# Float64 weights of a three-stage chain turned into float32 ahead of their pass and kept in main memory

## The chip, the cores and the metric

One core of one Trainium2 chip runs the whole program. The metric is the device time of one execution in microseconds (us). The time of the kernel before is the median of its runs shown below.

## What is computed

Three layers in a row. A retention layer comes first: for 4 batches and 8 heads, `scores = q k^T / 8`, times a decay matrix `gamma^(i-j)` on and below the diagonal, times `v`. Its output, reshaped to 2304 tokens by 512 columns, goes through two feed-forward layers:

```python
def _moe_ref(x, w_in, w_out):
    h = x @ w_in                    # 2304x512 @ 512x2048
    g = h * np.cos(h)
    return (g @ w_out).astype(np.float32)

def _moe2_ref(x, w_in, w_out):
    h = x @ w_in
    g = np.maximum(h, 0.0) + np.log1p(np.exp(-np.abs(h)))
    return (g @ w_out).astype(np.float32)
```

q, k and v are float32. The four weight matrices are float64. The engines have no float64 arithmetic, so the kernel has to turn every weight into float32 from its bits. Each float32 factor is then split into a high and a low part in TensorE's reduced float32 format, and a product is three matmuls: high by high, high by low, low by high.

## The kernel before, in words

**Weights.** A layer's 2048 hidden columns are 16 blocks of 128 (index `f`). A block has two tiles, `z = 0` (its columns of `w_in`) and `z = 1` (its rows of `w_out`), each 128 x 512 values, 512 KB in float64. `convert` (L327) makes one tile float32. A DMA (L339) brings the 512 KB into a buffer `wr`, of which there are three. ScalarE scales the high words into `wy` (L344). For layer 2 and for blocks 0 to 7 of layer 1, ScalarE also extracts the top bits of the low words (L350), and VectorE assembles the result in `wk` with two operations (L356, L363). For blocks 8 to 15 of layer 1, VectorE does it with three (L359, L363, L367). There are two buffers `wk` and one `wy`. Then ScalarE writes the high part, and VectorE or GpSimd subtracts to get the low part.

**First part (`moe_a`).** The attention is cut into 64 pieces. 16 of them run alone at the start; the others lie between the matmuls of the first feed-forward layer's blocks 0 to 7, which go over five groups of tokens (512, 512, 384, 384, 512). The weights of these blocks are converted one block at a time (`weight`, L380). Their partial sums go to main memory (`pd`).

**Second part (`moe_c`), three passes.** Pass 0 takes blocks 8 to 15 of layer 1, pass 1 blocks 0 to 7 of layer 2, pass 2 blocks 8 to 15 of layer 2. Each pass goes over the tokens in five pieces of 512, 512, 512, 512 and 256 (in an order of its own), and over its eight blocks as four pairs. `quad` (L832) computes two blocks at once by Strassen's scheme in Winograd's form: seven products of half size with sums and differences in PSUM (L890 to L898). `weight_pair` (L404) prepares a pair: four converted tiles (L428, L452), four combinations (L445), six splits into high and low (L424, L425, L453, L455). A pass's pair occupies the same SBUF slot as the pair of the same number in the pass before, so it can only be written once that pair has been used for the last time, and must be written before the new pass reaches it, four pairs later. The input `x` of a piece is loaded, combined and split by `x_load_c` (L1018), and in pass 1 its parts are stored for pass 2.

**Order.** Every operation is registered with a duration and a due time (`key`). `Plan.order` (L141) simulates the engines and takes, again and again, the operation that can start first; among those that can start at the same moment the smaller key goes first. That fixes each engine's program order. An operation marked "pool or dve" or "act or dve" goes to whichever engine gives the smaller start plus `FLEX` (or `FLEX_AD`) times duration (L178 to L186). A DMA is issued by SyncE (SP), in order, not before its key minus `LEAD` in the plan. Buffers of a ring (`wr`, `wk`, `tt`, and so on) are handed out in the order in which the operations were registered. The constants at the top (L68 to L108) set the keys: `W0` and `M0` for the start of the first part, `W2` and `W3` for pairs, `XC` for loads of `x`.

Of the kernel before, what the change touches and what calls it, by code (L numbers as in the profile page):

```python
# [7 lines left out]
F32 = mybir.dt.float32  # L8
F32R = mybir.dt.float32r
I32 = mybir.dt.int32  # L10
# [6 lines left out]
NF = DFF // 128  # L17
# [6 lines left out]
NM = len(GROUPS)  # L24
# [40 lines left out]
    return layer == 2 or f < FA  # L65


FLEX = 0.27  # L68
FLEX_AD = 0.824
NP = 3  # L70
RS = 5
WR = 3
# [1 line left out]
PT = 3  # L74
R0 = 22.0
WB = (21.627, 3.294)
W2 = (18.111, 6.589, 14.31, 1.214)
W3 = (16.671, 1.958)
XC = 3.809
LAG_C = 1.049  # L80
TT = 3
TURN = 0.6
XS = 60.0
FILL = (2, 5)
EARLY = 12.734
EARLY_2 = 8.236
AHEAD = {}
GAP = 2.0
LO_A = "pool or dve"
# [4 lines left out]
WARM = 350  # L94
DX = 20.621
LEAD = 7.381
W0 = (39.65, 2.003, 3.451)
M0 = 28.787
AK = (1.0, 2.2)
PAIR_A = 0.959  # L100
ALONE = 4
LENT = (0, 2)
SPREAD = (4, 6, 6)
# [141 lines left out]
def retention_moe_moe(ctx, tc, qkv, w1, w2, mask, mtail, dq, dk, out):  # L245
    nc = tc.nc
    pool = lambda name, bufs=1, **kw: ctx.enter_context(tc.tile_pool(name=name, bufs=bufs, **kw))
    dram = pool("dram", space=bass.MemoryType.DRAM)
    psum = pool("psum", 1, space=bass.MemoryType.PSUM)
    stage = pool("stage", 1)  # L250
# [18 lines left out]
    yd = dram.tile([128, NC, NT], F32, name="yd")  # L269
    sd = [dram.tile([128, len(CB), 7, 512], F32, name=f"sd{g}") for g in "hl"]  # L270
    od = dram.tile([NT, DM], F32, name="od")
    m_t = cst.tile([128, 4, 2, 128], F32, name="m_t")
    mt_t = cst.tile([128, 4, 64], F32, name="mt_t")
    dq_t = cst.tile([128, 4, 320], F32, name="dq_t")
# [2 lines left out]
    T = {}  # L277

    def dma(dst, src, nbytes, key, r=(), w=(), new=(), pre=None):
        def go():  # L280
            if pre:
                pre()
            nc.sync.dma_start(dst(), src())

        op("sp", 0.45, key, go, r, w, new, nbytes=nbytes)
# [41 lines left out]
    def convert(layer, f, z, k):  # L327
# [49 lines left out]
            op("dve", t_dve(512), k + 0.8, bits3, r=[rk, ak], w=[ak], port=True)  # L377
        return ak, lambda: T["wk", u].bitcast(F32)

    def weight(layer, f, key, step):  # L380
        wk = ("w", layer, f)
        for z in range(2):
            k = key + z * step
            ak, val = convert(layer, f, z, k)

            def hi(z=z, val=val):
                if z == 0:
                    T[wk] = tuple(wa_of(f).tile([128, 1024], F32R, tag=f"{g}{f}", name=g) for g in ("wh", "wl"))
                s = slice(z * 512, z * 512 + 512)
                nc.scalar.activation(T[wk][0][:, s], val(), AF.Copy)  # L390

            def lo(e, z=z, val=val):
                s = slice(z * 512, z * 512 + 512)
                sub(e, T[wk][1][:, s], val(), T[wk][0][:, s])

            th, tl = (wk, "h", z), (wk, "l", z)
            op("act", t_act(512), k + 2.2, hi, r=[ak], w=[th],
               new=[(f"w{f}", 1, wk)] if z == 0 else [])
            if LO_A == POOL_DVE:
                op(POOL_DVE, 512, k + 2.8, lo, r=[ak, th], w=[tl])  # L400
            else:
                op("pool", t_pool(512), k + 2.8, lambda lo=lo: lo(nc.gpsimd), r=[ak, th], w=[tl], port=True)

    def weight_pair(layer, q, key, step):  # L404

        slot_ = q % (NP2 // 2)
        wk = ("wp", layer, q)  # L410
        made = (wk, "made")

        def make():
            p = wp["qqrp"[slot_]].tile([128, 5632], F32R, tag=f"pair{slot_}", name="pair")
            T[wk] = p[:, 0:1792], p[:, 1792:3584]
            T[wk, "o"] = p[:, 3584:5632].rearrange("p (j g d) -> p j g d", j=2, g=2)

        op("host", 0.0, key, make, r=[("qqrp"[slot_] + "open",)], w=[made], new=[(f"wp{slot_}", 1, wk)])
        val, ak = [None, None], [None, None]
        part = lambda g, a, b: T[wk][g][:, a * 256:b * 256]  # L420

        def split(name, a, b, k, src, r):
            n = (b - a) * 256
            op("act", t_act(n), k, lambda: nc.scalar.activation(part(0, a, b), src(), AF.Copy), r=r + [made], w=[(wk, "h", name)])  # L424
            op(POOL_DVE, n, k + 0.6, lambda e: sub(e, part(1, a, b), src(), part(0, a, b)), r=r + [(wk, "h", name)], w=[(wk, "l", name)])  # L425

        for j in range(2):
            ak[j], val[j] = convert(layer, 2 * q + j, 0, key + j * step)  # L428
        k = key + step + 2.2
        split("a", 0, 2, key + 2.2, val[0], [ak[0]])  # L430
        split("b", 2, 3, k, lambda: val[1]()[:, 256:512], [ak[1]])
        tt = [("tt", wk, z) for z in range(2)]
        at = lambda i: T[tt[i // 2]][:, i % 2 * 256:i % 2 * 256 + 256]
        A = lambda: val[0]()
        Bv = lambda: val[1]()
        t_ = lambda i: (tt[i // 2], i % 2)
        for i, (x, y, o_, r) in enumerate((
                (lambda: Bv()[:, 0:256], lambda: Bv()[:, 256:512], ALU.add, [ak[1]]),
                (lambda: at(0), lambda: A()[:, 0:256], ALU.subtract, [ak[0], t_(0)]),
                (lambda: A()[:, 0:256], lambda: Bv()[:, 0:256], ALU.subtract, [*ak]),  # L440
                (lambda: A()[:, 256:512], lambda: at(1), ALU.subtract, [ak[0], t_(1)]))):
            def combine(e, x=x, y=y, o_=o_, i=i):
                if i % 2 == 0:
                    T[tt[i // 2]] = wp["q"].tile([128, 512], F32, tag="tt", name="tt", bufs=TT)
                e.tensor_tensor(at(i), x(), y(), o_)  # L445

            op(POOL_DVE, 256, k + 0.1 * i, combine, r=r + [("qopen",)], w=[t_(i)], new=[] if i % 2 else [("tt", TT, tt[i // 2])])
        for name, a in (("c", 3), ("d", 5)):
            split(name, a, a + 2, k + 0.6, lambda a=a: T[tt[a // 2 - 1]], [t_(a - 3), t_(a - 2)])
        for j in range(2):  # L450
            k = key + (2 + j) * step
            ok, ov = convert(layer, 2 * q + j, 1, k)  # L452
            op("act", t_act(512), k + 2.2, lambda j=j, ov=ov: nc.scalar.activation(T[wk, "o"][:, j, 0], ov(), AF.Copy),  # L453
               r=[ok, made], w=[(wk, "oh", j)])
            op(POOL_DVE, 512, k + 2.8, lambda e, j=j, ov=ov: sub(e, T[wk, "o"][:, j, 1], ov(), T[wk, "o"][:, j, 0]),  # L455
               r=[ok, (wk, "oh", j)], w=[(wk, "ol", j)])
# [657 lines left out]
    def moe_c(ph, y):  # L1114
# [9 lines left out]
        for m in range(n // 128 if ph else NC):  # L1124
# [20 lines left out]
            for i, (p, q) in enumerate(cuts):  # L1145
# [2 lines left out]
            dma(lambda r0=r0, m=m: out[r0:r0 + 128] if ph else yd[:, m, a:a + n], lambda pk=pk: T[pk], 512 * w, K + 1,  # L1148
                r=[(pk, i) for i in range(len(cuts))], w=[("out", r0) if ph else ("yd", m, b)])

    x_of[0, 0] = x_load_c(0, 0, CO[0][0], MB - XC)
    for q in range(half_p):
        weight_pair(1, half_p + q, M[NM - 2] + W2[0] + W2[1] * q if q < 2 else MB + q * UC(512) - W2[2], W2[3])
    for ph in range(3):
        if ph == 1:
            op("act", 1.3, CM[1][0], lambda: nc.scalar.preload_act_table_set("softplus"), r=[("sin",)], w=[("ln",)])
        if ph:
            x_of[ph, 0] = x_load_c(ph, 0, CO[ph][0], CM[ph][0] - XC)
            for q in range(half_p):
                weight_pair(2, q + (ph - 1) * half_p, CM[ph][0] + q * UC(512) - W3[0], W3[1])  # L1160
        for y in range(len(CB)):
            moe_c(ph, y)
    plan.emit(nc)
# [66 lines left out]
```

## Time and profile before

| | us |
|---|---|
| runs of the kernel before | 892.19, 896.02, 897.17 |
| median | 896.02 |
| the profiled execution, its own time | 892.48 |
| its span, first to last instruction | 890.7 |
| outside the span | 1.8 |

The profiled execution is one more execution than the three runs. Its span is cut into its parts by rows of the trace further down. In the profile, PE is TensorE's matmuls, PEld its weight loads, DVE VectorE, ACT ScalarE, POOL GpSimd, SP the queue that issues the DMAs. A granted clock of 1.00 is TensorE's full 2.4 GHz. In a row of matmuls, times in square brackets are the idle time of the engine before that row and what ended it.

### The profile page before, as it was taken

Reading aid. Unit: us, or ns where it says so; the run is one execution under the profiler, and the core shown is the slowest. Engines: PE = TensorE matmul, PEld = TensorE weight load, DVE = VectorE, ACT = ScalarE, POOL = GpSimd, SP = SyncE. Lnnn points to the kernel's source line nnn. Section 1 sums busy time; section 2 is a strip of 40 time slices with the busy share of each in tenths; the row PEclk is TensorE's granted clock in tenths of the full one; section 3 lists DMA queues with packets and bytes.
Section 4 is the critical chain, followed back from the end, with each engine's and each line's share of the span. In section 5 each row is a group of like instructions: output and inputs, shape, how many; then the busy total and the mean of one; then the engine's idle time right before and its main releaser. Section 6 shows DMA issues by size and latency. Waiting matters only on the chain.

```text
span 890.7 us, 15157 instructions
## 1 busy us (share of the span) xinstructions
PE 861.9 (97%) x5780; PEld 751.2 (84%) x5780; DVE 633.0 (71%) x1169; ACT 454.2 (51%) x897; POOL 170.2 (19%) x168
## 2 busy tenths in 40 slices
PE   7989999999999989999999889999999999999998
PEld 5767777899987878898888769889888888888887
DVE  3889655565499996667879996567668886565654
ACT  1469533435367865545768845335446752233322
POOL 4522000100041361113232160013003220000000
PEclk9999999999999999999999999999999999999999
DMA  9876332532256512345365607156525734421202
GB/s 321 349 243 234 108 116 98 186 111 95 89 191 198 197 48 95 95 132 176 95 249 172 194 24 309 37 226 237 220 100 214 270 126 158 164 98 71 95 29 78
DMA packets 56232, 139.13 MB, mean 156 GB/s; under 512 B 5088, under 2 KB 24672, under 8 KB 54112
## 3 DMA queue, kind: packets, MB, share of 16 engines
q1 hardware_dynamic: 56160, 138.18, 44.2%
q8 instruction: 45, 0.74, 0.3%
q14 instruction: 27, 0.22, 0.1%
HBM read 93.59 MB, written 44.56 MB: 155 GB/s over the span
## 4 chain that ended last, share of the span: by engine, by line
PE 75%; DVE 11%; DMA 5%; ACT 4%; issue 3%; SPq 1%; POOL 0%; DVEq 0%; POOLq 0%; ACTq 0%
PE acc L919 27%; PE acc L823 9%; PE o L857 8%; PE hb L857 7%; PE s L857 6%; PE ha L857 5%; PE ha L723 4%; PE hb L723 3%; PE o L636 2%; DMA wr<-in_w 2%; DVE wk L363 2%; DMA pt<-pd 1%; DVE pair L291 1%; PE s L559 1%; DVE wk L356 1%
## 5 line engine op out<-in xcount | busy, mean ns | idle before, releaser
L919 PE MATMUL acc<-pair,gh 128*128 128x512 f32 x576 | 180.8, 395 | 0.1
L919 PE MATMUL acc<-pair,gl 128*128 128x512 f32 x288 | 114.0, 396 | 2.1 <-DVE gl L291 2.1
L919 PEld LDWEIGHTS acc<-pair,gh 128*128 128x128 f32 x576 | 101.0, 189 | 16.5 <-ACT gh L802 0.6
L919 PE MATMUL acc<-gh,pair 128*128 128x512 f32 (+1 forms) x320 | 100.2, 370 | 0.3 <-ACT gh L802 0.3
L790 ACT ACTIVATE er<-er 128x512 f32<-128x512 f32 (+1 forms) x80 | 47.0, 588 | 91.0 <-DVE er L787 90.9
L857 PE MATMUL o<-xx,pair 128*128 128x256 f32 x320 | 79.4, 290 | 6.2 <-DVE o L898 3.8
L857 PE MATMUL o<-x,pair 128*128 128x256 f32 x328 | 79.8, 287 | 3.1 <-ACT cv L295 3.1
L857 PE MATMUL hb<-x,pair 128*128 128x256 f32 x328 | 78.6, 283 | 3.9 <-DVE hb L898 1.9
L857 PE MATMUL hb<-xx,pair 128*128 128x256 f32 x320 | 78.0, 286 | 0.1
L857 PEld LDWEIGHTS o<-xx,pair 128*128 128x128 f32 x320 | 57.4, 191 | 12.9 <-DVE o L898 7.1
L919 PEld LDWEIGHTS acc<-pair,gl 128*128 128x128 f32 x288 | 54.2, 188 | 16.0 <-DVE gl L291 3.4
L773 ACT ACTIVATE er<-er,hp_t 128x512 f32<-128x512 f32 (+2 forms) x80 | 54.1, 679 | 24.0 <-DVE er L770 23.1
L919 PEld LDWEIGHTS acc<-gh,pair 128*128 128x128 f32 x320 | 58.5, 188 | 9.1 <-ACT gh L802 0.5
L857 PEld LDWEIGHTS o<-x,pair 128*128 128x128 f32 x328 | 58.8, 192 | 7.8 <-ACT cv L295 4.1
L857 PEld LDWEIGHTS hb<-x,pair 128*128 128x128 f32 x328 | 57.6, 188 | 8.9 <-DVE hb L898 3.4
L823 PE MATMUL acc<-gh,wh 128*128 128x512 f32 (+1 forms) x160 | 60.4, 377 | 0.3 <-ACT gh L802 0.3
L857 PEld LDWEIGHTS hb<-xx,pair 128*128 128x128 f32 x320 | 56.4, 188 | 4.9 <-DVE hb L898 2.4
L823 PE MATMUL acc<-gl,wh 128*128 128x512 f32 (+1 forms) x160 | 59.2, 370 | 1.3 <-DVE gl L291 1.2
L919 PE MATMUL acc<-gl,pair 128*128 128x512 f32 (+1 forms) x160 | 59.3, 370 | 0.2 <-DVE gl L291 0.2
L823 PE MATMUL acc<-gh,wl 128*128 128x512 f32 (+1 forms) x160 | 58.9, 368 | 0.0
L857 PE MATMUL s<-x,pair 128*128 128x256 f32 x256 | 58.8, 282 | 0.0
L857 PE MATMUL ha<-x,pair 128*128 128x256 f32 x256 | 58.3, 280 | 0.0
(201 smaller groups left out, 2092.3 us busy)
## 6 DMA issues: line engine op xcount, KB each, us to landing
wr<-in_w SPq DMA_DIRECT2D x64, 512.0 KB, 3.6
raw<-in_qkv SPq DMA_DIRECT2D x12, 640.0 KB, 5.0
raw<-in_qkv SPq DMA_DIRECT2D x12, 512.0 KB, 6.0
od<-pt SPq DMA_DIRECT2D x18, 256.0 KB, 2.8
pt<-od SPq DMA_DIRECT2D x18, 256.0 KB, 3.4
out<-pt SPq DMA_DIRECT2D x18, 256.0 KB, 2.0
pt<-pd SPq DMA_DIRECT2D x16, 256.0 KB, 3.3
yd<-pt SPq DMA_DIRECT2D x16, 256.0 KB, 2.2
```

The source lines that it names most:

```text
L291: e.tensor_tensor(out_, a, hi.bitcast(F32), ALU.subtract)
L356: nc.vector.scalar_tensor_tensor(T["wk", u], T["wy", u], 3, T["wr", u][:, :, 0], ALU.logical_shift_left, ALU.bitwise_or)
L363: nc.vector.scalar_tensor_tensor(a, T["wy", u], -(1 << 31), a, ALU.bitwise_and, ALU.bitwise_or)
L559: nc.tensor.matmul(X()[j][:, z], k_(j, z), q_(z)[Z[j]], start=True, stop=True)
L636: nc.tensor.matmul(o_at(z)[Z[j]], lhs(j), rhs(j), start=start, stop=stop, skip_group_check=True)
L723: nc.tensor.matmul(h_[:, 0:n], lhs, rhs[:, d, 0:n], start=(k == 0), stop=(k == 3 * NC - 1))
L773: nc.scalar.activation(e["r"], e["r"], AF.Sin, bias=hp_t[:, 0:1], scale=-1.0)
L790: nc.scalar.activation(e["r"], e["r"], AF.Softplus)
L823: nc.tensor.matmul(acc[o][:, 0:n], l[:, s], e[r], start=(first and z == 0), stop=(last and z == 2))
L857: nc.tensor.matmul(out_, w_(a), x_(b), start=(start and y == 0), stop=(stop and y == 5), skip_group_check=True)
L919: nc.tensor.matmul(acc[m][:, 0:n] if layer == 1 else acc[m], l, r, start=(begin and z == 0), stop=(stop and z == 2))
```

## The change

Conversion and use of a tile come apart for ten pairs of blocks. A new helper `convert_ahead` converts a pair's four tiles with the same `convert`, and stores each as float32 in a new array `wd` in main memory (256 KB). A new helper `load_values` brings two such tiles at once (512 KB) into a `wr` buffer, and `weight_pair` takes the values from there if its new argument `ahead` is true. Done so are pairs 2 and 3 of pass 0 and all four pairs of pass 1, converted from the start of the second token group of the first part on (`M[1]`), one tile every 4.372 us by the keys, and all four pairs of pass 2, converted in pass 1, one tile every 5.526 us by the keys. Pairs 0 and 1 of pass 0 are converted at their place as before. Fourteen constants that set keys and the choice of engine get other values. The arithmetic is the same.

```diff
--- before.py
+++ after.py
@@ -65,8 +65,8 @@
     return layer == 2 or f < FA
 
 
-FLEX = 0.27
-FLEX_AD = 0.824
+FLEX = 0.317
+FLEX_AD = 1.075
 NP = 3
 RS = 5
 WR = 3
@@ -74,16 +74,17 @@
 PT = 3
 R0 = 22.0
 WB = (21.627, 3.294)
-W2 = (18.111, 6.589, 14.31, 1.214)
-W3 = (16.671, 1.958)
-XC = 3.809
-LAG_C = 1.049
+W2 = (29.96, 6.115, 14.31, 1.214)
+W3 = (16.671, 1.426)
+XC = 7.768
+LAG_C = 1.076
 TT = 3
+CA = (0.0, -5.457, 4.372, 5.526)
 TURN = 0.6
 XS = 60.0
 FILL = (2, 5)
-EARLY = 12.734
-EARLY_2 = 8.236
+EARLY = 12.574
+EARLY_2 = 6.751
 AHEAD = {}
 GAP = 2.0
 LO_A = "pool or dve"
@@ -94,10 +95,10 @@
 WARM = 350
 DX = 20.621
 LEAD = 7.381
-W0 = (39.65, 2.003, 3.451)
-M0 = 28.787
+W0 = (40.929, 2.003, 3.451)
+M0 = 28.434
 AK = (1.0, 2.2)
-PAIR_A = 0.959
+PAIR_A = 1.089
 ALONE = 4
 LENT = (0, 2)
 SPREAD = (4, 6, 6)
@@ -269,6 +270,7 @@
     yd = dram.tile([128, NC, NT], F32, name="yd")
     sd = [dram.tile([128, len(CB), 7, 512], F32, name=f"sd{g}") for g in "hl"]
     od = dram.tile([NT, DM], F32, name="od")
+    wd = dram.tile([2, NF, 2, 128, 512], F32, name="wd")
     m_t = cst.tile([128, 4, 2, 128], F32, name="m_t")
     mt_t = cst.tile([128, 4, 64], F32, name="mt_t")
     dq_t = cst.tile([128, 4, 320], F32, name="dq_t")
@@ -377,6 +379,28 @@
             op("dve", t_dve(512), k + 0.8, bits3, r=[rk, ak], w=[ak], port=True)
         return ak, lambda: T["wk", u].bitcast(F32)
 
+    def convert_ahead(layer, q, key, step):
+
+        for z in range(2):
+            for j in range(2):
+                f = 2 * q + j
+                k = key + (2 * z + j) * step
+                ak, val = convert(layer, f, z, k)
+                dma(lambda f=f, z=z: wd[layer - 1, f, z], lambda val=val: val(), 128 * 2048, k + 4, r=[ak], w=[("wd", layer, f, z)])
+
+    def load_values(layer, q, z, k):
+
+        u = (layer, q, z, "v")
+        rk = (("wr",) + u,)
+
+        def pre():
+            T["wr", u] = stage.tile([128, 512, 2], I32, tag="wr", name="wr", bufs=WR)
+
+        at = lambda: T["wr", u].rearrange("p a b -> p (a b)").bitcast(F32)
+        dma(lambda: at().rearrange("p (j d) -> p j d", j=2), lambda: wd[layer - 1, 2 * q:2 * q + 2, z].rearrange("j p d -> p j d"),
+            128 * 4096, k - 3.0, r=[("wd", layer, 2 * q + j, z) for j in range(2)], w=[rk], new=[("wr", WR, rk[0])], pre=pre)
+        return [rk] * 2, [lambda j=j: at()[:, j * 512:j * 512 + 512] for j in range(2)]
+
     def weight(layer, f, key, step):
         wk = ("w", layer, f)
         for z in range(2):
@@ -401,7 +425,7 @@
             else:
                 op("pool", t_pool(512), k + 2.8, lambda lo=lo: lo(nc.gpsimd), r=[ak, th], w=[tl], port=True)
 
-    def weight_pair(layer, q, key, step):
+    def weight_pair(layer, q, key, step, ahead):
 
 
 
@@ -424,8 +448,11 @@
             op("act", t_act(n), k, lambda: nc.scalar.activation(part(0, a, b), src(), AF.Copy), r=r + [made], w=[(wk, "h", name)])
             op(POOL_DVE, n, k + 0.6, lambda e: sub(e, part(1, a, b), src(), part(0, a, b)), r=r + [(wk, "h", name)], w=[(wk, "l", name)])
 
-        for j in range(2):
-            ak[j], val[j] = convert(layer, 2 * q + j, 0, key + j * step)
+        if ahead:
+            ak, val = load_values(layer, q, 0, key)
+        else:
+            for j in range(2):
+                ak[j], val[j] = convert(layer, 2 * q + j, 0, key + j * step)
         k = key + step + 2.2
         split("a", 0, 2, key + 2.2, val[0], [ak[0]])
         split("b", 2, 3, k, lambda: val[1]()[:, 256:512], [ak[1]])
@@ -447,9 +474,11 @@
             op(POOL_DVE, 256, k + 0.1 * i, combine, r=r + [("qopen",)], w=[t_(i)], new=[] if i % 2 else [("tt", TT, tt[i // 2])])
         for name, a in (("c", 3), ("d", 5)):
             split(name, a, a + 2, k + 0.6, lambda a=a: T[tt[a // 2 - 1]], [t_(a - 3), t_(a - 2)])
+        if ahead:
+            oks, ovs = load_values(layer, q, 1, key + 2 * step)
         for j in range(2):
             k = key + (2 + j) * step
-            ok, ov = convert(layer, 2 * q + j, 1, k)
+            ok, ov = (oks[j], ovs[j]) if ahead else convert(layer, 2 * q + j, 1, k)
             op("act", t_act(512), k + 2.2, lambda j=j, ov=ov: nc.scalar.activation(T[wk, "o"][:, j, 0], ov(), AF.Copy),
                r=[ok, made], w=[(wk, "oh", j)])
             op(POOL_DVE, 512, k + 2.8, lambda e, j=j, ov=ov: sub(e, T[wk, "o"][:, j, 1], ov(), T[wk, "o"][:, j, 0]),
@@ -1148,16 +1177,21 @@
             dma(lambda r0=r0, m=m: out[r0:r0 + 128] if ph else yd[:, m, a:a + n], lambda pk=pk: T[pk], 512 * w, K + 1,
                 r=[(pk, i) for i in range(len(cuts))], w=[("out", r0) if ph else ("yd", m, b)])
 
+    for i, (layer, q) in enumerate([(1, half_p + 2), (1, half_p + 3)] + [(2, q) for q in range(half_p)]):
+        convert_ahead(layer, q, M[1] + CA[0] + 4 * i * CA[2], CA[2])
     x_of[0, 0] = x_load_c(0, 0, CO[0][0], MB - XC)
     for q in range(half_p):
-        weight_pair(1, half_p + q, M[NM - 2] + W2[0] + W2[1] * q if q < 2 else MB + q * UC(512) - W2[2], W2[3])
+        weight_pair(1, half_p + q, M[NM - 2] + W2[0] + W2[1] * q if q < 2 else MB + q * UC(512) - W2[2], W2[3], q >= 2)
     for ph in range(3):
         if ph == 1:
             op("act", 1.3, CM[1][0], lambda: nc.scalar.preload_act_table_set("softplus"), r=[("sin",)], w=[("ln",)])
         if ph:
             x_of[ph, 0] = x_load_c(ph, 0, CO[ph][0], CM[ph][0] - XC)
             for q in range(half_p):
-                weight_pair(2, q + (ph - 1) * half_p, CM[ph][0] + q * UC(512) - W3[0], W3[1])
+                weight_pair(2, q + (ph - 1) * half_p, CM[ph][0] + q * UC(512) - W3[0], W3[1], True)
+            if ph == 1:
+                for q in range(half_p):
+                    convert_ahead(2, half_p + q, CM[1][0] + CA[1] + 4 * q * CA[3], CA[3])
         for y in range(len(CB)):
             moe_c(ph, y)
     plan.emit(nc)
```

## Rows read from the trace of the kernel before

**Rows 1.** the page, section 1: span, and each engine's busy time
```profile
span 890.7 us, 15157 instructions
PE 861.9 (97%) x5780; PEld 751.2 (84%) x5780; DVE 633.0 (71%) x1169; ACT 454.2 (51%) x897; POOL 170.2 (19%) x168
```

**Rows 2.** busy by stage: length; PE, PEld, DVE, ACT, POOL (xcount); clock; DMA share; GB/s
```profile
60.00:100.00 40.00, 39.25 (x213) 31.26 (x213) 36.51 (x67) 32.38 (x61) 7.63 (x7) 1.00 0.57 191
100.00:240.00 140.00, 140.00 (x1026) 122.90 (x1026) 75.45 (x177) 56.65 (x121) 7.41 (x11) 1.00 0.33 109
...
260.00:340.00 80.00, 75.84 (x427) 66.21 (x426) 75.99 (x129) 57.76 (x105) 28.38 (x24) 0.98 0.41 138
...
440.00:460.00 20.00, 18.12 (x114) 15.92 (x114) 16.83 (x24) 11.94 (x23) 10.81 (x9) 1.00 0.45 169
...
480.00:540.00 60.00, 53.50 (x308) 46.08 (x307) 57.57 (x90) 43.08 (x81) 21.61 (x21) 0.97 0.41 133
540.00:660.00 120.00, 120.00 (x766) 107.88 (x765) 78.52 (x134) 52.72 (x106) 14.68 (x10) 1.00 0.52 199
660.00:740.00 80.00, 77.44 (x471) 67.30 (x470) 67.46 (x112) 49.61 (x96) 20.11 (x18) 1.00 0.52 188
```

**Rows 3.** the same view, L363 alone (its time and count of VectorE), by stage
```profile
60.00:100.00 40.00, 7.52 (x11) 1.00 0.57 191
...
480.00:540.00 60.00, 8.55 (x11) 0.97 0.41 133
540.00:660.00 120.00, 1.36 (x2) 1.00 0.52 199
```

**Rows 4.** timeline of TensorE at stalls: start, duration, instruction, idle before
```profile
318.68 0.58 PE L857 MATMUL o<-x,pair 128*128 128x256 f32 x1 [2.74 <-ACT cv L295]
...
504.63 0.50 PE L919 MATMUL acc<-pair,gl 128*128 128x512 f32 x1 [1.57 <-DVE gl L291]
...
530.89 0.58 PE L857 MATMUL o<-xx,pair 128*128 128x256 f32 x1 [3.16 <-DVE o L898]
...
710.80 0.39 PE L857 MATMUL hb<-x,pair 128*128 128x256 f32 x1 [1.19 <-ACT cv L295]
```

**Rows 5.** timeline of VectorE ahead of two of these stalls
```profile
503.29 0.68 DVE L363 SCALAR_TENSOR_TENSOR wk<-wy,wk 128x512 int32<-128x512 int32 x1
...
525.69 1.78 DVE L363 SCALAR_TENSOR_TENSOR wk<-wy,wk 128x512 int32<-128x512 int32 x1
...
528.72 1.77 DVE L291 TENSOR_TENSOR pair<-wk,pair 128x512 fp32r<-128x512 f32 x1
530.41 0.42 DVE L898 TENSOR_TENSOR o<-o,c 128x256 f32<-128x256 f32 x1
```

**Rows 6.** timeline of GpSimd beside them
```profile
525.18 1.74 POOL L291 TENSOR_TENSOR xx<-tt,x 128x512 fp32r<-128x512 f32 x1
```

**Rows 7.** granted clock (after the engines' busy time) in 4 us stretches behind stalls
```profile
320.00:324.00 4.00, 4.00 (x22) 3.74 (x22) 3.12 (x7) 2.12 (x5) 2.90 (x3) 0.73 0.00 0
...
532.00:536.00 4.00, 4.00 (x17) 3.28 (x17) 3.14 (x7) 1.41 (x4) 0.00 (x0) 0.78 0.44 131
```

**Rows 8.** operations of a conversion: count, shortest/median/longest in ns, first and last start
```profile
L344 ACT ACTIVATE wy<-wr x64: 644/668/692, 36.2 to 722.6; 128x512 f32<-128x512 f32 x64
L350 ACT ACTIVATE wr<-wr x48: 650/673/720, 36.8 to 717.8; 128x512 int32<-128x512 uint8 x48
L356 DVE SCALAR_TENSOR_TENSOR wk<-wy,wr x48: 670/684/1680, 38.7 to 723.4; 128x512 int32<-128x512 int32 x48
...
L363 DVE SCALAR_TENSOR_TENSOR wk<-wy,wk x64: 672/683/1776, 39.4 to 724.3; 128x512 int32<-128x512 int32 x64
```

**Rows 9.** timeline of ScalarE and SP at two places
```profile
709.33 0.66 ACT L350 ACTIVATE wr<-wr 128x512 int32<-128x512 uint8 x1 [1.32 <-DMA wr<-in_w]
...
29.65 10.08 SPq L283 DMA_DIRECT2D wr<-in_w  x5
```

**Rows 10.** issues of DMAs: KB each, median us from issue to landing
```profile
wr<-in_w SPq DMA_DIRECT2D x64, 512.0 KB, 3.6
```

## The prediction

> **What bounds the kernel now.** I read the page first: TensorE is busy in 861.9 of a span of 890.7 us, so nothing can win more than what TensorE loses [rows 1]. Then I read busy time by stage, to see where it loses [rows 2]. From 100 to 240 us (the first part) and from 540 to 660 us (inside pass 1) it is busy for the whole stretch. It is idle at the changes of pass: 80 - 75.84 = 4.2 us from 260 to 340 (into pass 0), 60 - 53.50 = 6.5 us from 480 to 540 (into pass 1), 80 - 77.44 = 2.6 us from 660 to 740 (into pass 2), and 1.9 us from 440 to 460. VectorE is at 95%, 96% and 84% in the first three (75.99 of 80, 57.57 of 60, 67.46 of 80), against 54% and 65% in the two quiet stretches. So the kernel is bound by TensorE, and by VectorE where a pass begins. The start, up to 60 us, where attention runs alone, is hardly touched by the change.
>
> What stands in VectorE's queue at those places comes from the timelines. TensorE waits 1.57 us for `gl`, and a conversion (L363) is the operation just ahead of it; it waits 3.16 us for the addition L898, and ahead of that stands another L363 that took 1.78 us [rows 4, 5]. Into pass 0 it waits 2.74 us, into pass 2 1.19 us for a copy on ScalarE; ahead of the latter a conversion (L350) had itself waited for its weights to land [rows 4, 9]. After the two longest waits the granted clock is 0.73 and 0.78 over 4 us: TensorE, idle just before, runs part of the stretch at 1.2 instead of 2.4 GHz [rows 7]. That costs another 4 x 0.27 = 1.1 and 4 x 0.22 = 0.9 us.
>
> **The change, part by part.**
>
> *Removed at the changes of pass.* A tile of layer 2 costs ScalarE 0.67 + 0.67 and VectorE 0.68 + 0.68 us [rows 8]. From 480 to 540 there are 11 conversions, 11 x 1.37 = 15 us of VectorE's 57.6 [rows 3]; without them it stands near 42 of 60, 71%. Into pass 0 only pairs 2 and 3 (8 tiles) leave; pairs 0 and 1 stay and bunch as before.
> - Into pass 0 I take the 2.74 us wait and its clock loss, 2.74 + 1.1 = 3.8. The other 1.4 us of idle time stays.
> - Into pass 1 I take the two waits that have a conversion ahead of them and the clock loss, 1.57 + 3.16 + 0.9 = 5.6. The rest, 1.8 us, stays.
> - Into pass 2 I take all, 2.6 us, since nothing but weights is prepared there (pass 2 loads finished parts of x).
> - From 440 to 460 I take nothing: there the input of pass 1 is loaded.
>
> Together 12.0 us. The bounds are 0 (another operation takes each place) and all idle time of these stages with the clock losses, 4.2 + 1.9 + 6.5 + 2.6 + 2.0 = 17.2.
>
> *Added in the first part: 24 conversions.* 8 tiles of layer 1 (three VectorE operations; I use 0.68 for each, which is high for one of them) and 16 of layer 2 make 8 x 2.0 + 16 x 1.37 = 38 us on VectorE within 24 x 4.372 = 105 us, 36% on top of 54%: 90%. ScalarE gets 8 x 0.67 + 16 x 1.34 = 27 us, 26% on top of 40%. The cover is the slack between a block's activations and its output matmuls. The nearest row is the stretch from 60 to 100 us, where the same code converts 11 tiles beside the same matmuls, with VectorE at 36.51 of 40, 91% [rows 2, 3]. TensorE is idle there 0.75 us, so at most 0.75/11 = 0.07 us per tile; the lower bound is 0. I take the upper, 24 x 0.07 = 1.6 us, as the load is as high.
>
> *Added in pass 1: 16 conversions.* 16 x 1.37 = 22 us on VectorE over 16 x 5.526 = 88 us, 25% on top of 65%, again 90%. Two conversions already lie in that stretch at no idle time [rows 2, 3]. I take 0.07 again: 1.1 us. Without cover each operation would cost TensorE its 0.68 us; that is a rival below.
>
> *Added DMAs: 40 stores of 256 KB and 20 loads of 512 KB, 21 MB in all.* The 64 loads from the inputs stay, but 40 of them move. In the first part the conversions bring 24 x 0.75 MB in 105 us, 180 GB/s on top of 109, where the queue is busy at 0.33; the stretch from 60 to 100 carries 191 at 0.57 [rows 2]. At the changes of pass a pair now needs two loads instead of four, each 3.6 us by the row of the old ones [rows 10]: a gain, in the sum above. SP issues in order, so behind a store that waits for its conversion stand attention's inputs (issued 22 us early), the partial sums `pd` and the `xd` stores, for which three buffers `pt` wait. I cost that at 0: an input has 22 us, and SP has gaps. If the cover is gone, an accumulator is emptied late, which is in the slower rival.
>
> *Keys.* `W0` delays the first weight loads by 1.28 us. The first is issued at 29.65 us [rows 9], and its key minus 3 minus `LEAD` is 39.65 - 3 - 7.38 = 29.27, so this delay will show; but a block's matmuls come only behind the attention that runs alone. I take 0, with 1.3 either way. `FLEX` shifts flexible subtractions from GpSimd to VectorE, `XC` brings x 4 us earlier, pairs 0 and 1 of pass 0 come 12 us later but wait for x's buffers anyway. The trace of before cannot price these; 2 us either way, and 0 taken.
>
> **Sum.** -12.0 + 1.6 + 1.1 = -9.3 us. The profiled execution took 892.48 us, 1.8 more than its span. The runs took 892.19, 896.02 and 897.17. The four fall in two pairs, so I put the sum on the middle of the four, (892.48 + 896.02)/2 = 894.25, which is 1.8 below the median: 894.3 - 9.3 = 885.0 us.
>
> **A rule against part of it.** While GpSimd runs an x subtraction of 1.74 us, VectorE's operations take 1.78 instead of 0.68 us: L363, but also the pair's subtraction (L291, 1.77), which the change does not remove [rows 5, 6]. The Trainium skill, page "SBUF — State Buffer", section "Who interferes with whom", says that a VectorE instruction with two SBUF inputs contends with a GpSimd instruction that reads SBUF, and that the one who comes second is blocked fully. The trace agrees: 1.1 us lost each time. By that rule taking out conversions leaves the other collisions, which is the first rival.
>
> **Rivals.**
> - *The collisions stay.* Splits and x loads still meet GpSimd's work. Then each of the two long waits shrinks only by one collision, 1.1 us, the 1.57 us wait by two conversions of 0.68 (1.4), the clock losses stay, and pass 2 gains its 2.6: 6.2 - 2.7 = 3.5 us, 890.8. For it: two of the four long operations around the 3.16 us wait are not conversions. Against it: with VectorE at 71% the queue has gaps that absorb 1.1 us. Chance 0.20.
> - *The conversions don't get away from the change of pass.* Tiles of pass 2 follow pass 1's pairs in the `wr` ring. Pair 3's last load is due at 2 x 1.426 + 3 x 10.47 - 16.67 = 17.6 us after the pass begins (10.47 is the plan's time for a pair, L309), the first conversion at -5.5. So four tiles are late by then, and with older keys than the pass's own work they go first, in a burst where VectorE was full. Then the 5.6 us are not won: 3.7 us, 890.6. Against it: a burst of 4 is less than the 11 there now. Chance 0.10.
> - *Slower: conversions break the chain of the first part.* Until the third group ends only two PSUM banks hold the hidden values (L962), and matmul, activation, split and output matmul follow each other closely. If every one of the 40 tiles puts one operation of 0.68 us in front of that chain, or a late store holds `pd`, the cost is 40 x 0.68 = 27 us, less 12.0: 894.3 + 15.2 = 909.5. It turns slower by over 0.5% when a tile costs TensorE more than (12.0 + 900.5 - 894.3)/40 = 0.46 us. Against it: 0.07 in the row. For it: in that row the converted tiles were needed at once; here 24 extra ones come on top of pieces of attention with their own deadlines. Chance 0.13.
>
> **How the numbers follow.** The forecast has 0.57. 0.5% is 4.5 us, about what a measurement of this kernel can tell from no change: faster is below 891.5, slower above 900.5. The two rivals near 890.7 hold 0.30; with the spread of the runs 0.18 of it counts as faster and 0.12 as within 0.5%. Of the slower rival 0.11 ends above 900.5 and 0.02 within. So faster 0.75, same 0.14, slower 0.11. The range reaches down to the bound of all idle time won, 894.3 - 17.2 - 1 (part of the keys' 2) = 876, and up past the small-gain rivals by the spread of the runs, to 895; the slower rival is left out.
>
> **What would show it.** Right: by stage, L363's time disappears from 480 to 540 and 660 to 740 and appears between 90 and 210; TensorE's idle time there falls from 6.5 to about 2 and from 2.6 to about 0; the clock stays at 1.00 behind the change of pass; the first part, 100 to 240, stays within 2 us of full. Wrong: a stall at L898 or `cv` with VectorE operations of 1.7 us beside GpSimd (first rival); L363 bunched in the first 40 us of pass 1 (second); matmuls L723 or L823 waiting for VectorE, or evictions waiting for `pt`, in the first part (third).

## The result, and the profile after

The changed kernel takes 883.9 us (median of 7 runs, 882.68 to 889.66) against 894.56 (7 runs, 892.19 to 897.17): a ratio of 0.9889, 95% interval 0.986 to 0.9918. The forecast was 885.0 us, faster, in a range from 876 to 895.

The traced execution of the changed kernel is the slowest of its seven (889.66 us), while that of the kernel before (892.48) lies below its median. So the two traces differ by 2.8 us where the medians differ by 10.7: what the traces show place by place is real, but they cannot be added up to the whole gain.

The page, section 1, of the changed kernel (answers to [rows 1]):

```profile
span 887.9 us, 15301 instructions
PE 865.3 (97%) x5780; PEld 751.1 (85%) x5780; DVE 630.7 (71%) x1179; ACT 454.4 (51%) x892; POOL 171.1 (19%) x163
```

Busy time by stage, columns as in [rows 2]:

```profile
100.00:240.00 140.00, 137.71 (x989) 118.80 (x988) 102.47 (x224) 80.30 (x161) 6.76 (x9) 0.98 0.68 232
260.00:340.00 80.00, 78.71 (x442) 67.81 (x441) 66.60 (x115) 53.94 (x101) 29.65 (x25) 1.00 0.36 122
...
480.00:540.00 60.00, 57.34 (x346) 50.04 (x345) 50.67 (x78) 37.60 (x69) 28.13 (x22) 0.97 0.68 236
540.00:660.00 120.00, 119.01 (x743) 105.82 (x743) 84.90 (x148) 59.06 (x115) 17.92 (x13) 1.00 0.60 219
660.00:740.00 80.00, 79.50 (x491) 70.22 (x490) 58.17 (x92) 36.79 (x72) 15.47 (x14) 1.00 0.42 154
```

At the changes of pass TensorE's idle time falls from 4.16 to 1.29, from 6.50 to 2.66 and from 2.56 to 0.50 us. In the first part it rises from 0 to 2.29, with VectorE at 102 instead of 75 us and the DMA share at 0.68 instead of 0.33.

The last operation of a conversion (L363 before, L365 now) alone, its VectorE time and count by stage (answers to [rows 3]):

```profile
100.00:240.00 140.00, 17.98 (x26) 0.98 0.68 232
480.00:540.00 60.00, 6.17 (x7) 0.97 0.68 236
540.00:660.00 120.00, 7.31 (x10) 1.00 0.60 219
660.00:740.00 80.00, 0.00 (x0) 1.00 0.42 154
```

**What was lost in the first part.** The chain of waits, 128 to 153 us (start, duration, what):

```profile
128.66 4.91 DMA wr<-in_w
...
136.43 6.03 DMA wd<-wk
...
142.72 9.69 DMA wd<-wk
...
152.51 0.70 DVE wk L358
...
153.24 0.69 DVE wk L365
153.93 0.61 DVE er L792
```

The timelines of SP, ScalarE and TensorE at that place, in this order:

```profile
141.56 0.33 SPq L285 DMA_DIRECT2D wr<-in_w  x1
...
151.78 0.67 ACT L352 ACTIVATE wr<-wr 128x512 int32<-128x512 uint8 x1 [3.67 <-DMA wr<-in_w]
152.35 0.58 ACT L788 ACTIVATE ek<-ha 128x512 int32<-128x512 f32 x1
...
157.16 0.50 PE L852 MATMUL acc<-gh,wh 128*128 128x512 f32 x1 [1.90 <-ACT gh L831]
158.06 0.50 PE L852 MATMUL acc<-gl,wh 128*128 128x512 f32 x1 [0.40 <-DVE gl L293]
```

And what the stretches around it carry (columns as in [rows 2]):

```profile
145.00:150.00 5.00, 5.00 (x24) 4.13 (x23) 3.32 (x8) 2.22 (x5) 0.25 (x1) 1.00 1.03 404
...
155.00:160.00 5.00, 2.71 (x11) 1.53 (x10) 3.98 (x8) 3.35 (x6) 0.00 (x0) 0.92 0.82 283
160.00:165.00 5.00, 5.00 (x33) 3.73 (x33) 3.96 (x10) 3.09 (x7) 0.87 (x1) 0.50 0.79 231
165.00:170.00 5.00, 5.00 (x44) 4.09 (x42) 3.42 (x7) 2.38 (x5) 0.00 (x0) 0.89 0.88 300
```

Stores of finished tokens `x`, attention's inputs and conversions fall together; the queue is full (share 1.03, 404 GB/s). The load of weights issued at 141.56 us lands 10.2 us later, and the 256 KB store issued at 142.72 takes 9.69 us. Two engines stop for them, each in its own program order. ScalarE stands 3.67 us before a conversion's L352, until the weights have landed, with the `ek` of a block (L788) queued behind it. VectorE cannot run a conversion's L358 before the store has freed a buffer `wk`, and the same block's `er` (L792) is queued behind that conversion. VectorE's is the later of the two, and the chain of waits goes through it. TensorE waits 1.90 and 0.40 us for that block's `gh` and `gl`, which is all its idle time from 155 to 160 us and in the whole first part (2.29). Then it runs from 160 to 165 us at 0.50, that is 1.2 GHz: 5 x 0.50 = 2.5 us more.

**What stayed at the change of pass.** The timelines of VectorE, GpSimd and TensorE there (answer to [rows 4 to 6]):

```profile
513.36 1.78 DVE L293 TENSOR_TENSOR xx<-tt,x 128x512 fp32r<-128x512 f32 x1
515.06 1.74 DVE L365 SCALAR_TENSOR_TENSOR wk<-wy,wk 128x512 int32<-128x512 int32 x1
516.72 0.42 DVE L927 TENSOR_TENSOR hb<-hb,c 128x256 f32<-128x256 f32 x1
...
514.55 1.71 POOL L293 TENSOR_TENSOR xx<-tt,x 128x512 fp32r<-128x512 f32 x1
...
517.20 0.39 PE L886 MATMUL hb<-xx,pair 128*128 128x256 f32 x1 [2.02 <-DVE hb L927]
```

One stall of 2.02 us is left. Its conversion is one of the tiles of pass 2. Its two slow VectorE operations, 1.78 and 1.74 instead of 0.68 us, lie beside GpSimd operations (one of 1.62 us, then the one shown, 1.71). The Trainium skill, page "SBUF — State Buffer", section "Who interferes with whom", has a VectorE instruction with two SBUF inputs contend with a GpSimd instruction that reads SBUF; the trace agrees again.

DMA issues (KB each, median us from issue to landing; answers to [rows 10]):

```profile
wr<-in_w SPq DMA_DIRECT2D x64, 512.0 KB, 4.9
wd<-wk SPq DMA_DIRECT2D x40, 256.0 KB, 4.4
wr<-wd SPq DMA_DIRECT2D x20, 512.0 KB, 3.7
```

### The profile page after: what moved, and what is told of

It is laid out like the page before. It is cut to its first block, busy times and chain, and to the rows that moved or that the text cites. A ratio compares the mean times of both kernels' runs of the same rounds, so it can differ in the third digit from the quotient of the medians.

```text
span 887.9 us, 15301 instructions
## 1 busy us (share of the span) xinstructions
PE 865.3 (97%) x5780; PEld 751.1 (85%) x5780; DVE 630.7 (71%) x1179; ACT 454.4 (51%) x892; POOL 171.1 (19%) x163
## 4 chain that ended last, share of the span: by engine, by line
PE 70%; DVE 13%; DMA 7%; ACT 5%; issue 3%; SPq 1%; POOL 1%; DVEq 0%; POOLq 0%; ACTq 0%
PE acc L948 28%; PE o L886 8%; PE hb L886 7%; PE acc L852 6%; PE s L886 6%; PE ha L886 5%; PE ha L752 2%; DMA wd<-wk 2%; PE hb L752 2%; DVE wk L365 2%; DMA wr<-in_w 2%; DVE wk L358 1%; DVE pair L293 1%; DVE gl L293 1%; DVE er L792 1%
## 5 line engine op out<-in xcount | busy, mean ns | idle before, releaser
L346 ACT ACTIVATE wy<-wr 128x512 f32<-128x512 f32 x64 | 42.8, 669 | 31.2 <-DVE wk L365 26.2
```

Source lines behind the costliest of these rows:

```text
L346: nc.scalar.activation(y, T["wr", u][:, :, 1].bitcast(F32), AF.Copy, scale=2.0 ** -112)
```

## The experiments

Short diffs go from the changed kernel. Since one execution is traced and executions differ by some us, each run has two readings: the median, and the length of each stage of its trace. The stage lengths below (us) run from start to start of the first matmul of a kind, so they are worked out from rows of TensorE's timeline: A from the first block matmul of the first layer to the fifth token group, B from there to the first `quad`, then pass 0 up to the first output matmul of layer 2, pass 1 to the middle of layer 2's output matmuls, and pass 2 to the last of them.

```
                  median  ratio   95%              A      B     0      1      2
before            894.56  1                      188.5  41.1  217.3  200.1  188.3
after             883.9   0.9889 0.986-0.9918    195.8  40.3  211.2  200.2  185.1
e1_keys_only      898.15  1.0041 1.0025-1.0057   189.3  43.0  217.7  201.5  187.4
e2_old_keys       892.59  0.9987 0.9975-1.0      192.1  44.3  214.9  196.8  185.1
e3_first_six      883.64  0.9887 0.9852-0.9921   192.8  40.3  212.0  195.2  187.0
e4_pass2_only     899.57  1.0068 1.0044-1.0092   189.4  43.0  217.7  205.3  185.1
e5_late           885.41  0.9892 0.9866-0.9917   193.9  40.3  210.0  196.4  185.1
e6_double_store   897.57  1.0038 1.0017-1.0059   201.5  40.3  211.0  200.9  185.1
e7_double_dve     907.84  1.0151 1.0125-1.0178   203.3  40.3  211.5  207.7  185.1
e9_spread         886.88  0.9914 0.9892-0.9937   190.6  40.3  211.1  198.2  185.6
e8_old_but_two    888.35  0.9928 0.9901-0.9954   192.7  40.3  212.0  197.3  185.7
e10_new_but_two   886.91  0.9925 0.9897-0.9953   192.0  43.5  211.2  196.9  185.1
e11_split         882.5   0.9868 0.9841-0.9895   189.4  40.3  211.3  196.5  185.1
e12_split_six     883.18  0.9874 0.9846-0.9901   189.9  40.3  212.4  195.3  187.3
```

B and pass 0 must be read together where the order differs. In `e1_keys_only`, `e4_pass2_only` and `e10_new_but_two` the first `quad` stands later in TensorE's program: 12 output matmuls of the first part follow it there, 24 in all other runs. These 12 take 12 x 0.23 = 2.8 us, which B has more and pass 0 less without any time lost.

Ratios are against the kernel before on the same chip, whose median there was 893.9 to 894.6 us.

### Keys without conversions ahead, and the reverse

`e1_keys_only` has the new constants alone:

```diff
-... in enumerate([(1, half_p + 2), (1, half_p + 3)] + [(2, q) for q in range(half_p)]):
+... in enumerate([]):
...
-... W2[3], q >= 2)
+... W2[3], False)
...
-... W3[1], True)
-            if ph == 1:
+... W3[1], False)
+            if ph == 9:
```

> The new constants alone; no tile is converted ahead, all are converted at their place. Theory (the gain comes from taking conversions out of the changes of pass): 893 to 897 us, TensorE idle about 6 us again around the change into pass 1, VectorE above 90% there. Rival (the newly chosen keys bring it): 884 to 887 us.

Measured: 1.0041 (1.0025 to 1.0057). The new constants by themselves make it slower, 898.15 us, which is above the 893 to 897 us of the theory and far from the rival's. One stage of its trace (columns as in [rows 2]) has more idle time than before, 7.3 against 6.5 us:

```profile
480.00:540.00 60.00, 52.70 (x300) 44.99 (x299) 57.59 (x92) 43.93 (x83) 22.19 (x20) 0.97 0.38 128
```

`e2_old_keys` keeps the conversions ahead and `CA`, with every other constant of the change as before. By the diff of the change these are eleven constants with twelve values, not fourteen:

```diff
-FLEX = 0.317
+FLEX = 0.27
-W2 = (29.96, 6.115, 14.31, 1.214)
+W2 = (18.111, 6.589, 14.31, 1.214)
...
-XC = 7.768
+XC = 3.809
```

> The conversions ahead as in the changed kernel, but all fourteen constants but the new ones for the conversions' own due times (CA) set back to those of before. Theory: 884 to 888 us, as the work has moved all the same. Rival (keys): 893 us or more. If the structure needs its keys, it lies in between, and the trace shows at which stage.

Measured: 892.59 us, 0.9987 (0.9975 to 1.0), almost no gain, between its two ranges and next to the rival's 893. The traces say where it differs from the whole change: B is 44.3 instead of 40.3 us and pass 0 is 214.9 instead of 211.2. Timelines of VectorE and TensorE there:

```profile
282.21 1.78 DVE L369 SCALAR_TENSOR_TENSOR wk<-wr,wk 128x512 int32<-128x512 int32 x1
283.91 0.94 DVE L361 TENSOR_SCALAR wk<-wy 128x512 int32<-128x512 int32 x1
284.78 0.68 DVE L293 TENSOR_TENSOR gl<-hb,gh 128x512 fp32r<-128x512 f32 x1
...
285.51 0.50 PE L852 MATMUL acc<-gl,wh 128*128 128x512 f32 x1 [2.19 <-DVE gl L293]
```

With the old keys, conversions of pass 0's own pairs still stand ahead of `gl` where the first part ends. TensorE's idle time from 260 to 340 us is 4.49 us, as much as before, while from 480 to 540 it is 1.88 and from 660 to 740 it is 0.96: with the old keys the conversions ahead cut TensorE's idle time into passes 1 and 2, not into pass 0. Neither half gains; together they gain 1.1%. Constants and structure do not add.

### Which pair of constants

`e8_old_but_two` is `e2_old_keys` with `W2` and `XC` new; `e10_new_but_two` is the changed kernel with only these two old:

```diff
-W2 = (29.96, 6.115, 14.31, 1.214)
+W2 = (18.111, 6.589, 14.31, 1.214)
...
-XC = 7.768
+XC = 3.809
```

> Conversions ahead, the constants of before except two: W2 (due times of pass 0's pairs) and XC (how early x is loaded) are the new ones. Theory (the old due times cost the earlier run with old constants its gain at the beginning of pass 0, where its stages were 7.7 us longer than the changed kernel's): 884 to 888 us. Rival (another constant, FLEX or EARLY, does it): 891 to 893 us, as with all old constants.

> The changed kernel with W2 and XC alone set back to before. Theory: 889 to 893 us, the loss at the beginning of pass 0. Rival: 883 to 886 us.

Measured: 888.35 us, 0.9928, just above its theory, and 886.91 us, 0.9925, between its two ranges. From either side these two are worth a third to a half of the 8.7 us between `e2_old_keys` and the change: 892.59 - 888.35 = 4.2 us added to the old constants, 886.91 - 883.9 = 3.0 taken from the new ones. In the traces it is B and pass 0 together: 44.3 + 214.9 = 259.2 us with both old against 40.3 + 212.0 = 252.3 in `e8_old_but_two`, and 43.5 + 211.2 = 254.7 in `e10_new_but_two` against 40.3 + 211.2 = 251.5 with the whole change. In the trace of `e10_new_but_two` TensorE stalls as pass 0 begins, one row by stage and four of its timeline:

```profile
260.00:340.00 80.00, 75.67 (x419) 64.73 (x418) 67.02 (x112) 52.10 (x97) 22.89 (x18) 0.98 0.34 109
```
```profile
296.91 0.38 PE L886 MATMUL o<-x,pair 128*128 128x256 f32 x1 [1.24 <-ACT cv L297]
300.90 0.38 PE L886 MATMUL o<-x,pair 128*128 128x256 f32 x1 [0.89 <-DVE o L927]
306.19 0.50 PE L948 MATMUL acc<-gh,pair 128*128 128x512 f32 x1 [1.29 <-ACT gh L831]
307.35 0.50 PE L948 MATMUL acc<-gl,pair 128*128 128x512 f32 x1 [0.66 <-DVE gl L293]
```

Idle time there is 4.33 us, before's level [rows 2], with pairs 2 and 3 long converted. `W2` and `XC` were not tried apart, nor which of the other constants carries the rest.

### Which conversions ahead pay

`e3_first_six` leaves pass 2's tiles to be converted at their place; `e4_pass2_only` converts those alone ahead:

```diff
 e3_first_six
-... W3[1], True)
-            if ph == 1:
+... W3[1], ph == 1)
+            if ph == 9:
 e4_pass2_only
-... in enumerate([(1, half_p + 2), (1, half_p + 3)] + [(2, q) for q in range(half_p)]):
+... in enumerate([]):
...
-... W2[3], q >= 2)
+... W2[3], False)
...
-... W3[1], True)
+... W3[1], ph == 2)
```

> Ahead only what the first part converts (pairs 2 and 3 of pass 0, the four of pass 1); pass 2's pairs are converted at their place. Theory, by the terms of the forecast: 894.5 - 3.8 - 5.6 + 1.6 = 886.7 us, and TensorE's idle time into pass 2 as before (2 to 3 us). Rival (small gains, collisions stay): 891 to 893 us.

> Ahead only pass 2's four pairs, converted in pass 1. Theory, by the terms of the forecast: 894.5 - 2.6 + 1.1 = 893 us; the first part has no idle TensorE from 100 to 240 us and the change into pass 1 is as crowded as before or more. Rival (the conversions in pass 1 land on its beginning): above 895 us.

Measured: 883.64 us, 0.9887, the ratio of the whole change and 3 us better than its theory; and 899.57 us, 1.0068, on its rival's side and no better than the keys alone (1.0041, the intervals overlap). So the six pairs of the first part carry the gain, and those of pass 2 give nothing net: in `e4_pass2_only` pass 2 is 187.4 - 185.1 = 2.3 us shorter than with the keys alone, and pass 1 is 205.3 - 201.5 = 3.8 us longer. Pass 1 of `e3_first_six`, by stage:

```profile
480.00:540.00 60.00, 58.75 (x364) 51.63 (x363) 46.14 (x72) 33.24 (x63) 22.79 (x20) 1.00 0.37 136
540.00:660.00 120.00, 120.00 (x751) 107.01 (x750) 72.50 (x124) 53.90 (x106) 17.96 (x14) 1.00 0.47 176
```

Without pass 2's conversions beside it the change of pass has 1.25 us of idle time instead of 2.66, and pass 1 none behind it.

### Pass 2's conversions later in pass 1

```diff
-CA = (0.0, -5.457, 4.372, 5.526)
+CA = (0.0, 40.0, 4.372, 5.526)
```

> The changed kernel with one number moved: the conversions for pass 2 fall due 40 us after pass 1 begins, not 5.5 us before. Theory (these conversions cost TensorE only where they meet x's splits at the beginning of pass 1): the 2.0 us wait near 515 us goes, pass 1 is 2 to 4 us shorter, 880 to 883 us. Rival (they cost the same anywhere in pass 1, as VectorE is near 90% with them): no change, 883 to 886 us.

Measured: 885.41 us, 0.9892, the same as the change and in the rival's range, although its trace has pass 1 at 196.4 us and no stall at the place of the 2.02 us one. As one trace is not the median, a gain of 1 to 2 us can neither be shown nor excluded.

### What the first part costs: transfers or VectorE

`e6_double_store` stores every tile that is converted ahead a second time, to an array that nobody reads; `e7_double_dve` issues one VectorE operation of each such conversion twice, with the same result. The plan knows of neither, so the order stays:

```diff
 e6_double_store
...
             nc.sync.dma_start(dst(), src())
+            if also:
+                nc.sync.dma_start(also(), src())
...
 e7_double_dve
...
-            nc.vector.scalar_tensor_tensor(a, T["wy", u], -(1 << 31), a, ALU.bitwise_and, ALU.bitwise_or)
+            for _ in range(2 if twice else 1):
+                nc.vector.scalar_tensor_tensor(a, T["wy", u], -(1 << 31), a, ALU.bitwise_and, ALU.bitwise_or)
...
```

> The changed kernel, each converted tile stored twice, the second time into an array that nobody reads; the order of all else is the same. That adds 40 stores of 256 KB. Theory A (what the conversions cost in the first part comes through full DMA queues: weights that land late stop ScalarE's and VectorE's queues): the first part grows by 3 us or more, 887 to 895 us. Theory B (it comes from VectorE's load): the first part stays, 883 to 886 us.

> The changed kernel, with the second VectorE operation of each conversion ahead (L363 of before) done twice, the same result: 24 x 0.68 = 16 us more of VectorE in the first part, 11 us more in pass 1; no byte more is moved. Theory A (DMA): the first part is within 2 us of the changed kernel's, 884 to 888 us. Theory B (VectorE's load): the first part loses 4 us or more, over 888 us.

Measured: 897.57 us, 13.7 more than the changed kernel, and 907.84, 23.9 more: the first lies above both of its ranges, the second in that of theory B. By stage, `e6_double_store` first:

```profile
100.00:240.00 140.00, 132.46 (x951) 112.04 (x950) 102.92 (x220) 78.11 (x158) 7.02 (x9) 0.98 0.79 277
```
```profile
100.00:240.00 140.00, 131.71 (x939) 110.00 (x938) 118.59 (x246) 79.05 (x159) 7.58 (x9) 0.98 0.68 232
...
480.00:540.00 60.00, 54.05 (x322) 46.88 (x321) 55.45 (x84) 40.03 (x75) 30.57 (x24) 0.97 0.60 196
540.00:660.00 120.00, 115.82 (x710) 101.23 (x709) 94.52 (x159) 57.38 (x112) 20.87 (x14) 1.00 0.60 221
```

Idle time in the first part goes from 2.29 to 7.54 us with more transfers and the same VectorE load, and to 8.29 with more VectorE and the same transfers. So adding to either costs TensorE time there. How the loss of the changed kernel itself divides between the two does not follow from these runs; its chain of waits above names the late transfers. Nor does `e6_double_store` fill the queue alone: a buffer `wk` is also held until its second store has landed, and from 100 to 240 us VectorE waits 6.8 us in 5 waits for that, against 1.7 us in 2 waits for the one store of the changed kernel. The 40 added VectorE operations are 40 x 0.68 = 27 us, and 23.9 of it reached the end: added VectorE work is hardly hidden any more, in the first part or in pass 1. So the prediction's slower rival is a real mechanism one operation per tile away from the changed kernel.

### Conversions of the first part spread out

`e9_spread` only takes a wider step there:

```diff
-CA = (0.0, -5.457, 4.372, 5.526)
+CA = (0.0, -5.457, 5.0, 5.526)
```

> The changed kernel with one number moved: the conversions of the first part fall due every 5.0 us instead of every 4.372. Theory A (DMA): fewer bytes per us where the stores of x lie, the long waits near 155 us become shorter, 881 to 884 us. Rival: the last tiles now push pairs 0 and 1 of pass 0 back, 885 us or more.

Measured: 886.88 us, 0.9914 (0.9892 to 0.9937), not faster than the change and in the rival's range. Its trace does have the first part shorter, by 195.8 - 190.6 = 5.2 us against the changed kernel's slowest execution and by 1.4 to 3.3 against the other traces with a step of 4.372 and nothing doubled:

```profile
100.00:240.00 140.00, 139.20 (x1011) 120.39 (x1010) 108.80 (x234) 80.62 (x163) 7.11 (x9) 1.00 0.68 235
```

`e11_split` moves 8 of the 24 tiles (pairs 2 and 3 of pass 1) into the quiet middle of pass 0, spaces the remaining 16, and takes pass 2's late; `e12_split_six` is that without pass 2 ahead (the two edits of `e3_first_six`):

```diff
-CA = (0.0, -5.457, 4.372, 5.526)
+CA = (0.0, 40.0, 6.5, 5.526)
...
-... in enumerate([(1, half_p + 2), (1, half_p + 3)] + [(2, q) for q in range(half_p)]):
+... in enumerate([(1, half_p + 2), (1, half_p + 3), (2, 0), (2, 1)]):
...
+    for i, q in enumerate((2, 3)):
+        convert_ahead(2, q, MB + 60.0 + 4 * i * 7.0, 7.0)
     for ph in range(3):
```

> The changed kernel with less in the first part: pairs 2 and 3 of pass 1 are converted in pass 0 (from 60 us after it begins, one tile every 7 us), so the first part has 16 tiles, one every 6.5 us; pass 2's conversions fall due 40 us into pass 1. Theory (the first part loses 2 to 7 us to conversions, VectorE and DMA queues both being near full there): 878 to 882 us, the first part within 2 us of before. Rival (what the first part wins pass 0 gives back): 883 to 886 us.

> As the run before, but pass 2's pairs are converted at their place. Theory, since pass 2's conversions ahead gained nothing in an earlier pair of runs: the same time as the run before within 1.5 us. Rival: 2 us longer, the idle time into pass 2.

Measured: 882.5 us, 0.9868 (0.9841 to 0.9895), between its two ranges, and 883.18, 0.9874, as its theory has it. The first part of `e11_split` is full again:

```profile
100.00:240.00 140.00, 140.00 (x1021) 122.21 (x1021) 96.55 (x214) 74.01 (x151) 8.18 (x12) 1.00 0.54 188
```

Its 95% interval overlaps that of the change, so the lowest median of all is not shown to be a gain over it, only to be no loss of size. That `e12_split_six` comes within 0.7 us of it agrees with `e3_first_six`: pass 2 ahead wins 187.3 - 185.1 = 2.2 us in pass 2 and costs 196.5 - 195.3 = 1.2 in pass 1.

## Why the prediction was right, point by point

**Right: what bounds the kernel and what leaves.** Conversions stood in VectorE's queue at the changes of pass, and taking them away took most of the stalls into passes 1 and 2 with either set of keys. Into pass 0 the 2.74 us stall is gone with the old `W2` and `XC` too, but others ahead of it bring the idle time back to 4.33 us (`e10_new_but_two`): the term of 3.8 us, put down to pairs 2 and 3 alone, needs the new keys as well. Into pass 0 and pass 1 the forecast was 3.8 + 5.6 = 9.4 us; in the trace of `e3_first_six` passes 0 and 1 are (217.3 - 212.0) + (200.1 - 195.2) = 10.2 us shorter. Into pass 2 it was 2.6; in the changed kernel's trace its stage is 188.3 - 185.1 = 3.2 us shorter, of which 188.3 - 187.4 = 0.9 come with the keys alone.

**Mis-sized: the first part.** "24 x 0.07 = 1.6" was taken from the stretch from 60 to 100 us because VectorE's load is as high there. The traces show 7.3 (its slowest execution), 4.3, 5.4 and 2.1 us more in A (after, e3, e5, e9). In the first of them one place holds most of it: 2.29 us idle and 2.5 + 5 x 0.11 = 3.1 us of clock. The row had the right VectorE load but a DMA share of 0.57. Its one pair of large `x` stores (issued at 82.32 and 82.94 us) came behind its last load of weights, and it stored no converted tile. The step that failed is "I cost that at 0: an input has 22 us, and SP has gaps": the waiting party was not an input but the conversions' own operations, on ScalarE for weights that landed late and on VectorE for a buffer that a late store held, with a block's activation behind both. With 16 tiles at a step of 6.5 (`e11_split`) A is 0.9 us longer, 0.06 per tile, and the term is right as it was.

**Mis-sized: pass 1.** The forecast was 1.1 us for its 16 conversions; the traces show 200.2 - 195.2 = 5.0 and 198.2 - 195.2 = 3.0 where they start with the pass (after and e9 against e3) and 1.2 where they start late (e5 against e3, e11 against e12). The second rival was half right: it was no burst (7 from 480 to 540 us in the rows of L365 above), but the earliest ones did come where VectorE was still needed.

**Wrong: the keys.** "2 us either way, and 0 taken" priced them apart from the structure. Alone they cost 898.15 - 894.03 = 4.1 us, and the structure alone gains 894.03 - 892.59 = 1.4: added up, 2.7 us slower. Together they are 10.7 us faster, so 13 us come only from having both. Of the 892.59 - 883.9 = 8.7 us that the new constants bring to the structure, `W2` and `XC` hold 3 to 4. The reason given, that pairs 0 and 1 "wait for x's buffers anyway", does not bear the 0: with `W2` and `XC` old, B and pass 0 together are 254.7 - 251.5 = 3.2 us (e10 against after) and 259.2 - 252.3 = 6.9 us (e2 against e8) longer. That 885.0 came out so close to 883.9 is partly luck, because errors went opposite ways: the passes gained about what was forecast, the first part and pass 1 cost more in the traces, and the keys were not the separate zero that they were taken for.

**Rivals.** The collisions stayed at one place and cost 2.02 us and a clock of 0.70 over 516 to 520, not the whole of the two waits; the late conversions went as said above; the slower rival did not decide. One of its signs did show: TensorE waits 2.18 us at 180.6 (`e3_first_six`) and 1.27 us at 178.3 (`e5_late`) for ScalarE's copy of an accumulator into `pt`; the changed kernel's own trace has no such wait. And doubling one operation brought 0.60 us per tile (23.9/40), above the 0.46 from which it was to decide.

**Open.** No execution of the changed kernel near its median was traced, so it is not shown how much of the 7.3 us in the first part a usual execution loses. The other runs with the same 24 tiles at the same step, and nothing doubled, have 3.5 to 5.4 us more in A than the kernel before (e2, e3, e5, e8, e10). A third `wk` buffer, which would let a store be late without stopping a later conversion, was not tried.

## What to carry to other kernels

Work that is moved out of a crowded stage must be priced at its new place by every resource that it uses there, with a row that has the same load on each of them: here VectorE's load matched and the transfer queue's did not. An operation that waits for a transfer, on an engine with a fixed program order, puts whatever stands behind it on that transfer's clock. When a change brings structure and constants together, run each alone before giving either a price: here one half lost 0.4%, the other gained 0.1%, and the pair gained 1.1%.

## What was unexpected of the hardware

A 256 KB store, 4.4 us in the median of 40, took 9.69 us, and a 512 KB load, 4.9 us in the median of 64, took 10.2 us, while the DMA share was 1.03 at 404 GB/s.

TensorE's clock at the start differs between executions of nearly the same work. From 20 to 30 us (columns as in [rows 2]), the kernel before, then `e3_first_six`:

```profile
20.00:30.00 10.00, 10.00 (x180) 7.97 (x180) 7.66 (x28) 2.53 (x10) 6.74 (x12) 1.00 1.03 412
```
```profile
20.00:30.00 10.00, 10.00 (x134) 7.76 (x130) 5.42 (x21) 1.38 (x5) 5.99 (x10) 0.70 0.97 371
```

TensorE is busy throughout in both, at 1.00 and at 0.70, and the first block matmul starts at 51.2 and 54.1 us. Over all traces here that start lies between 50.7 and 54.4 us, and the changed kernel, whose keys there are those of `e3_first_six`, starts it at 51.0. So some 3 us of the spread between executions are made in the first 50 us. Over the seven executions of the changed kernel the time follows the mean granted clock of the execution, from 882.68 us at 0.998 over 883.9 at 0.996 to 889.66 at 0.991. The kernel before has 0.992 in the median of 22 executions, so part of the gain, by an estimate 884 x 0.004 = 3.5 us of the 10.7, is a clock that falls less.
